# Moving two gate rows and eight modulation columns from TensorE to VectorE and GpSimd in a fused attention and MLP block

## The chip, the cores and the metric

The kernel runs on one core of one Trainium2 chip. The metric is the device time in microseconds (us) of one execution, here the median over several. Most executions agree within 0.3%. One execution of the kernel before took 1975.29 us, a single outlier that no ratio uses. All runs told of here are of the undisturbed state (the records show a mean granted TensorE clock of 1.00, and where a run has less it is said).

## The reference

A block with six modulation vectors made from a condition `c`, attention over the last 512 keys with 32 query heads and 8 key heads, then a two-layer MLP. x is 2048 x 512. Cut to what matters:

```python
mod = (silu(c) @ w_mod).reshape(6, 512)      # sa, ca, ga, sb, cb, gb: slices 0 to 5
h = layernorm(x) * (1 + ca) + sa
x = x + ga * attention(h, k_cache, v_cache, wq, wo)     # softmax over 512 keys
h = layernorm(x) * (1 + cb) + sb
x = x + gb * (relu(h @ w1) @ w2)
```

Slices 0 and 1 are needed at once. Slice 2 (the first gate, a row), slices 3 and 4 (the second modulation, four columns each of 128 partitions) and slice 5 (the second gate, a row) are needed only much later. Those four are what the change is about.

## The kernel before

The 2048 rows are 4 blocks (`NB`) of 512. The main loop has 128 steps, one for each block and head (32 heads to a block, `H`). A step of TensorE work is: scores of this head (psS), queries of a later head (psQ), the product of probabilities and values of the last head (psO, 16 matmuls), and up to four matmuls from a background queue (psW: output projection, and in steps 4 to 6 the modulation). `P` is 128, `DC` and `TPB` are 4.

```python
def mod_row(j):                       # a gate row, on all partitions: 4 matmuls of 512 columns
    sl, dst, r = (2, gaf, R_ga) if j == 0 else (5, gbf, R_gb)
    for cc in range(DC):
        bgq.append(lambda cc=cc: mm(bank[WBK], sc_rep[:, cc, :], wm[sl][:, cc, :], cc == 0, cc == DC - 1, [R_screp, R_wm[sl]], [WBK], cc == DC - 1))
    evac(lambda: kb.op(DVE, lambda e: e.tensor_copy(dst[:, :], bank[WBK]), reads=[R_b[WBK]], writes=[r]))

def mods2():                          # put into the background queue at step 4
    mod_row(0)
    fs = mod_cols_mm(1, WBK)          # slices 3 and 4: 32 matmuls of one column
    bgq.append(lambda: [f() for f in fs] and None)
    evac(lambda: mod_cols_evac(1, WBK))
    mod_row(1)

for s in range(NU):                   # NU = 128 steps
    run_tasks(s, 100)                 # side tasks that were placed at this step
    if s == 4:
        mods2()
    # ... (put an output projection into the queue when 8 heads are done)
    s_mms(s, 0)
    if s + QA < NU:
        q_mms(s + QA)
    s_mms(s, 1)
    if s >= 1:
        pv_mms(s - 1)
    pop_bg(4)
```

VectorE has to empty psO at each step, in program order with all else it does. TensorE can't start the next psO block before (in the trace after, psO blocks stood 3.2 us in all for it):

```python
def pv_mms(u):
    # ... 16 matmuls into o_ps, banks 5 and 6
    kb.op(DVE, lambda e: e.reciprocal(rinv[:, u, :], o_ps[:, :, P]), reads=[R_b[5], R_b[6]], writes=[R_rinv])
    kb.op(DVE, lambda e: e.tensor_tensor(o_sb[u % NOS][:, :, :], o_ps[:, :, 0:P], rinv[:, u, :].unsqueeze(2).to_broadcast([P, TPB, P]), op=ALU.mult),
          reads=[R_b[5], R_b[6], R_rinv], writes=[R_o[u % NOS]])
    # ... DMA transpose of o_sb to oT
```

The layer norms of blocks 1 to 3 and the second layer norms of blocks 0 to 2 are side tasks over some twelve steps each. They share one buffer `xn` (normalised rows) and one buffer `xnT` (the same, transposed by a DMA):

```python
xn = T("xn", [P, TPB, D])
xnT = T("xnT", [P, TPB, DC, P])

def add_ln(b, which, s0):
    dst, r = (hT[b % 2], R_hT[b % 2]) if which == 1 else h2_of[b]
    for tl in range(TPB):
        add(s0 + tl, lambda t=b * TPB + tl: ln_stat(t))               # DVE
    add(s0 + TPB, lambda: ln_rstd(b))                                 # DVE add, POOL power
    for tl in range(TPB):
        add(s0 + TPB + 1 + tl // 2, lambda t=b * TPB + tl: ln_norm(t))  # DVE: xn
    add(s0 + TPB + 2, ln_dmaT)                                        # DMA: xnT <- xn
    for cc in range(DC):
        add(s0 + TPB + 5 + cc // 2, lambda cc=cc: ln_mod_sb(cc, dst, r, which))  # DVE: hT <- xnT

for b in range(1, NB):
    # ...
    add_ln(b, 1, H * b - 15)          # steps 17 to 27, 49 to 59, 81 to 91
for b in range(NB - 1):
    add_ln(b, 2, H * (b + 1) + 19)    # steps 51 to 61, 83 to 93, 115 to 125
```

Of the kernel before, what the change touches and what calls it, by code (L numbers as in the profile page):

```python
# [3 lines left out]

# [2 lines left out]

ACTF = mybir.ActivationFunctionType
ALU = mybir.AluOpType
AX = mybir.AxisListType  # L10
BF = mybir.dt.bfloat16
F32 = mybir.dt.float32
# [1185 lines left out]
def build_fast(nc, es, top, A_x, A_k_cache, A_v_cache, A_wq, A_wo, B_x, B_w1, B_w2, c, w_mod, out, flag):  # L1198
    P = 128
    _, Sq, D = A_x.shape  # L1200
# [10 lines left out]
    DC = D // P  # L1211
# [15 lines left out]
    def T(name, shape, dt=BF):  # L1227
        return es.enter_context(nc.sbuf_tensor(name, shape, dt))
# [9 lines left out]
    h2T = [T(f"h2T{i}", [P, DC, QB]) for i in range(2)]  # L1238
# [7 lines left out]
    wm = [wm01[:, :, 0:D], wm01[:, :, D:2 * D]] + [wmw[:, i * DC * D:(i + 1) * DC * D].rearrange("p (c n) -> p c n", c=DC) for i in range(2, 6)]  # L1246
# [7 lines left out]
    ident = T("ident", [P, P])  # L1254
    ones = T("ones", [P, P])
    c_row = T("c_row", [DC, P])
    s3 = T("s3", [P, 4], F32)
    sc_bf = T("sc_bf", [P, DC])
    sc_rep = T("sc_rep", [P, DC, P])
    tmp = T("tmp", [P, DC], F32)  # L1260
    modc = T("modc", [P, 4 * DC], F32)
    gaf = T("gaf", [P, D], F32)
    gbf = T("gbf", [P, D], F32)
    st = T("st", [P, NT, 6], F32)
    mv = T("mv", [P, NT, 2], F32)
    rstd = T("rstd", [P, NT], F32)
    cst = T("cst", [P, 4], F32)
# [9 lines left out]
    bank = [s_ps[0][:, 0, :], s_ps[0][:, 1, :], s_ps[1][:, 0, :], s_ps[1][:, 1, :], q_ps[:, :],  # L1277
            o_ps[:, 0:2, :].rearrange("p a b -> p (a b)"), o_ps[:, 2:4, :].rearrange("p a b -> p (a b)"), w_ps[:, :]]
    QBK, WBK = 4, 7

    sem = lambda name: top.enter_context(nc.semaphore(name))
    kb = KB(nc)
    PE = kb.stream("pe", sem("s_pe"))
    ACT = kb.stream("act", sem("s_act"))
    DVE = kb.stream("dve", sem("s_dve"))
    POOL = kb.stream("pool", sem("s_pool"))
# [13 lines left out]
    RL = lambda name, n: [Res(f"{name}{i}") for i in range(n)]  # L1300
# [4 lines left out]
    R_acc, R_wm, R_w1, R_w2 = RL("acc", TPB), RL("wm", 6), RL("w1", FC), RL("w2", FC)  # L1305
    R_xn, R_xnT = RL("xn", TPB), Res("xnT")
    R_yt, R_yo = RL("yt", NY), RL("yo", NY)
    R_b = RL("bank", 8)
    R_ident, R_ones, R_c, R_sc, R_screp, R_tmp, R_cst = (Res(n) for n in ("ident", "ones", "c", "sc", "screp", "tmp", "cst"))
    R_moda, R_modb, R_ga, R_gb = Res("moda"), Res("modb"), Res("ga"), Res("gb")  # L1310
    R_st, R_mv, R_rstd = RL("st", NT), RL("mv", NT), RL("rstd", NT)
    R_s3, R_eps = Res("s3"), Res("eps")
    R_rinv, R_vmax, R_chk, R_good, R_flag = Res("rinv"), Res("vmax"), Res("chk"), Res("good"), Res("flag")
# [31 lines left out]
    def wm_res(sl, cc):  # L1345
        return R_wm[cc // (DC // 2)] if sl < 2 else R_wm[sl]
# [15 lines left out]
    def mm(out_ap, lhsT, rhs, start, stop, reads, bk, signal):  # L1362
        kb.op(PE, lambda e: e.matmul(out_ap, lhsT, rhs, start=start, stop=stop), reads=reads, group_writes=[R_b[k] for k in bk], signal=signal)  # L1363
# [66 lines left out]
    def mod_cols_mm(which, bk):  # L1430
        fs = []
        for idx, sl in enumerate((0, 1) if which == 0 else (3, 4)):
            for c2 in range(DC):
                for cc in range(DC):
                    last = idx == 1 and c2 == DC - 1 and cc == DC - 1
                    fs.append(lambda sl=sl, c2=c2, cc=cc, col=idx * DC + c2, last=last: mm(
                        bank[bk][:, col:col + 1], wm[sl][:, cc, c2 * P:(c2 + 1) * P], sc_bf[:, cc:cc + 1],
                        cc == 0, cc == DC - 1, [R_sc, wm_res(sl, cc)], [bk], last))
        return fs

    def mod_cols_evac(which, bk):
        mo, r = which * 2 * DC, (R_moda, R_modb)[which]
        kb.op(DVE, lambda e: e.tensor_copy(modc[:, mo:mo + DC], bank[bk][:, :DC]), reads=[R_b[bk]], writes=[r])
        kb.op(DVE, lambda e: e.tensor_scalar(modc[:, mo + DC:mo + 2 * DC], bank[bk][:, DC:2 * DC], 1.0, None, op0=ALU.add), reads=[R_b[bk]], writes=[r])

    def mod_row(j):
        sl, dst, r = (2, gaf, R_ga) if j == 0 else (5, gbf, R_gb)
        for cc in range(DC):
            bgq.append(lambda cc=cc: mm(bank[WBK], sc_rep[:, cc, :], wm[sl][:, cc, :], cc == 0, cc == DC - 1, [R_screp, R_wm[sl]], [WBK], cc == DC - 1))
        evac(lambda: kb.op(DVE, lambda e: e.tensor_copy(dst[:, :], bank[WBK]), reads=[R_b[WBK]], writes=[r]))  # L1450

    bgq = deque()

    def pop_bg(n):
        while bgq and (n > 0 or bgq[0] in evacs):
            f = bgq.popleft()
            f()
            n -= 1
            if f in evacs:
                break  # L1460
# [3 lines left out]
    def evac(f):  # L1464
        evacs.add(f)
        bgq.append(f)

    def q_mms(u, bk=QBK):
        b, h = units[u]
        order = CC_ORDER if u < QA else range(DC)  # L1470
        for i, cc in enumerate(order):
            mm(bank[bk], wq_sb[:, cc, h * Dh:(h + 1) * Dh], hT[b % 2][:, cc, :], i == 0, i == DC - 1,
               [R_wq[h], R_hT[b % 2][cc]], [bk], i == DC - 1)
        kb.op(ACT, lambda e: e.activation(qT[u % NQT][:, :], bank[bk], ACTF.Copy), reads=[R_b[bk]], writes=[R_qT[u % NQT]])  # L1474

    def s_mms(u, pr):
        b, h = units[u]
        g = h // R
        for i in range(2):
            kc = pr * 2 + i  # L1480
            mm(s_ps[pr][:, i, :], kT_sb[:, g, kc * P:(kc + 1) * P], qT[u % NQT][:, :], True, True, [R_kT[g], R_qT[u % NQT]], [kc], i == 1)
        kb.op(ACT, lambda e: e.activation(PT[u % NPT][:, pr * 2:pr * 2 + 2, :], s_ps[pr][:, :, :], ACTF.Exp, scale=scale),  # L1482
              reads=[R_b[pr * 2], R_b[pr * 2 + 1]], writes=[R_PT[u % NPT][pr]])
# [18 lines left out]
    def enqueue_wo(b, j):  # L1502
        for tl in range(TPB):
            t = b * TPB + tl
            for i in range(HQ):
                h = j * HQ + i
                slot = (b * H + h) % NOT
                bgq.append(lambda i=i, h=h, slot=slot, tl=tl: mm(bank[WBK], oT[slot][:, tl, :], wo_sb[:, h, :], i == 0, i == HQ - 1,
                                                                [R_oT[slot], R_wo[j]], [WBK], i == HQ - 1))

            def fin(tl=tl, t=t):
                if j == 0:
                    kb.op(DVE, lambda e: e.tensor_copy(acc[:, tl, :], bank[WBK]), reads=[R_b[WBK]], writes=[R_acc[tl]])
                else:
                    kb.op(DVE, lambda e: e.tensor_tensor(acc[:, tl, :], bank[WBK], acc[:, tl, :], op=ALU.add), reads=[R_b[WBK], R_acc[tl]], writes=[R_acc[tl]])  # L1515
                if j == NPASS - 1:
                    eng = DVE if b == NB - 1 else POOL
                    kb.op(eng, lambda e: e.tensor_tensor(acc[:, tl, :], acc[:, tl, :], gaf[:, :], op=ALU.mult), reads=[R_acc[tl], R_ga], writes=[R_acc[tl]])  # L1518
                    kb.op(eng, lambda e: e.tensor_tensor(x_sb[:, t, :], acc[:, tl, :], x_sb[:, t, :], op=ALU.add), reads=[R_acc[tl], R_x[t]], writes=[R_x[t]])
                    x1_done.append(t)  # L1520
            evac(fin)
# [5 lines left out]
    def add(step, fn):  # L1527
        tasks.append((step, len(tasks), fn))
        tasks.sort(key=lambda x: x[:2])

    def run_tasks(step, n):
        while tasks and tasks[0][0] <= step and n > 0:
            tasks.pop(0)[2]()
            n -= 1
# [53 lines left out]
    for tl in range(3):  # L1588
# [3 lines left out]
          reads=[R_x[t3], R_rstd[t3], R_s3], writes=[R_xn[t3]])  # L1592
    fs = mod_cols_mm(0, QBK)
# [12 lines left out]
    load_v(1)  # L1606
    q_mms(0)
    q_mms(1, 5)
    kb.op(DVE, lambda e: e.tensor_copy(sc_rep[:, :, :], sc_bf[:, :].unsqueeze(2).to_broadcast([P, DC, P])), reads=[R_sc], writes=[R_screp])


    for g in range(2, G):
# [1 line left out]
    for g in range(G):  # L1614
        for i, op in enumerate((ALU.max, ALU.min)):
            add(max(R * g, 3), lambda g=g, i=i, op=op: kb.op(DVE, lambda e: e.tensor_reduce(vmax[:, i, g:g + 1], v_sb[:, g, :, 0:Dh], axis=AX.XY, op=op),
                                                             reads=[R_v[g]], writes=[R_vmax]))
# [9 lines left out]
    for i, s in enumerate([s for s in range(57, NU) if s % HQ in (1, 2, 3, 4)][:FC]):  # L1627
        add(s, lambda i=i: load_mlp(i))

    def mods2():  # L1630
        mod_row(0)
        fs = mod_cols_mm(1, WBK)
        bgq.append(lambda: [f() for f in fs] and None)
        evac(lambda: mod_cols_evac(1, WBK))
        mod_row(1)

    for s in range(NU):
        run_tasks(s, 100)
        if s == 4:
            mods2()  # L1640
        if wo_ready and wo_ready[0][0] <= s:
            _, b_, j_ = wo_ready.popleft()
            enqueue_wo(b_, j_)
# [7 lines that stand above are left out]
# [100 lines left out]
def bass_adaLN_cond__sliding_block_cached__dense_activation_relu__prompt_kernel(  # L1751
# [14 lines left out]
    with ExitStack() as top:  # L1766
        flag = top.enter_context(nc.sbuf_tensor("flag", [1, 8], mybir.dt.int32))
        with ExitStack() as es:
            kb, fast, cut, dma_cnt, flag_ev = build_fast(nc, es, top, *args, flag)
            sems = dict(kb.sems)  # L1770
            meet = top.enter_context(nc.semaphore("s_meet"))
# [71 lines left out]
```

## Time and profile before

| what | kernel before |
|---|---|
| median of 3 executions, us (all: 564.13, 1975.29, 563.9) | 564.13 |
| span in the profile, us | 562.5 |
| TensorE busy | 553.7 us, 98% |
| VectorE idle while it waits for psO | 233.1 us |
| GpSimd busy | 38.7 us, 7% |
| packets on queue 8, which the page lists as instruction | 35 |

Times are taken from outside and are some 1.7 us longer than the span. The prediction below quotes the main lines and says how to read them. In short: the chain is the path that ended last, and a saving counts only if the work lies on it; a group line ends with how long its engine was idle ahead of it, and after the arrow with what ended that. The view is the waits of the kernel before (engine, tile and line, what it waited for, then us in total, times, the longest):

```profile
DVE hT L1392 <- DMA xnT<-xn: 9.2, 3, 4.3
...
DVE xn L1384 <- DMA xnT<-xn: 4.5, 2, 2.2
```

The one of 4.3 us is the last layer norm, behind the loop. The other four, 2.2 to 2.5 us each, lie in blocks 2 and 3, and they cost TensorE nothing: the list has no wait of a psO block for VectorE.

### The profile page before, as it was taken

The page shows a single profiled execution, that of the slowest core. Times are in us where ns is not written, and L with a number is a line of the kernel's source. Part 1 is how long each engine was busy: PE and PEld are TensorE (multiplying, and loading weights), DVE is VectorE, ACT ScalarE, POOL GpSimd, SP SyncE. Part 2 cuts the span into 40 slices and gives each one's busy share as a digit, 9 for nine tenths or more (in the row PEclk, how much of TensorE's full clock was granted, in tenths as well). Part 3 has the DMA queues.
Part 4 walks back from the last instruction along what each step waited for, and adds up shares of the span by engine and source line. Part 5 has one row for each costly group of instructions (what it writes and reads, how often), then busy time and mean ns, then how long its engine had stood idle before and what let it go on. Part 6 is the DMA issues. An engine that isn't in the chain of part 4 may idle for free.

```text
span 562.5 us, 9700 instructions
## 1 busy us (share of the span) xinstructions
PE 553.7 (98%) x4097; PEld 316.9 (56%) x4172; DVE 242.2 (43%) x533; ACT 350.4 (62%) x453; POOL 38.7 (7%) x42
## 2 busy tenths in 40 slices
PE   8999999999999999999999999999999999999998
PEld 3565555555555555555555555555555654444444
DVE  4444465533334655333346553333354448321134
ACT  5986666666666666666666666666666644432500
POOL 1000000003300000033000000330000000000000
PEclk9999999999999999999999999999999999999999
DMA  9778776421331247332523522121123220210001
GB/s 268 204 165 167 143 160 132 113 38 38 39 76 37 39 93 133 57 94 46 144 56 57 102 50 39 39 40 40 39 39 72 44 31 0 41 36 24 22 28 48
DMA packets 113310, 42.70 MB, mean 76 GB/s; under 512 B 93928, under 2 KB 112104, under 8 KB 113256
## 3 DMA queue, kind: packets, MB, share of 16 engines
q1 hardware_dynamic: 112024, 40.82, 35.2%
q10 hardware_dynamic: 1232, 1.15, 0.6%
q8 instruction: 35, 0.57, 0.5%
q14 instruction: 19, 0.16, 0.1%
HBM read 18.35 MB, written 2.10 MB: 36 GB/s over the span
## 4 chain that ended last, share of the span: by engine, by line
PE 97%; issue 1%; DMA 1%; DVE 1%
PE psS L1363 28%; PE psO L1363 26%; PE psQ L1363 23%; PE psW L1363 20%; DMA x<-in_A_x_dram 1%; DVE st L1373 0%; PE psS L1366 0%; DVE mv L1374 0%; DVE rstd L1574 0%; DVE PT L1673 0%; DVE PT L1675 0%; DVE tmp L1427 0%; DVE sc_bf L1428 0%; DVE tmp L1426 0%
## 5 line engine op out<-in xcount | busy, mean ns | idle before, releaser
L1482 ACT ACTIVATE PT<-psS 128x1024 bf16<-128x1024 f32 x256 | 262.6, 1028 | 129.5 <-PE psS L1363 129.4
L1363 PE MATMUL psS<-qT,kT 128*128 128x512 bf16 x509 | 151.1, 379 | 0.2
L1363 PEld LDWEIGHTS psO<-v,PT 128*128 128x128 bf16 x2048 | 126.6, 98 | 30.2
L1363 PE MATMUL psO<-v,PT 128*128 128x129 bf16 x2048 | 137.0, 220 | 0.0
L1363 PE MATMUL psQ<-hT,wq 128*128 128x512 bf16 x507 | 130.3, 379 | 0.1
L1492 DVE RECIPROCAL rinv<-psO 128x4 f32<-128x4 f32 x128 | 23.4, 183 | 233.1 <-PE psO L1363 233.1
L1363 PE MATMUL psW<-wo,oT 128*128 128x512 bf16 x451 | 117.9, 379 | 3.2
L1493 DVE TENSOR_TENSOR o<-psO,rinv 128x512 bf16<-128x512 f32 x128 | 88.5, 692 | 4.4
L1363 PEld LDWEIGHTS psQ<-hT,wq 128*128 128x128 bf16 x508 | 49.6, 98 | 60.7 <-issue 0.5
L1363 PEld LDWEIGHTS psS<-qT,kT 128*128 128x128 bf16 x512 | 49.6, 98 | 59.3 <-ACT PT L1482 0.7
L1474 ACT ACTIVATE qT<-psQ 128x512 bf16<-128x512 f32 x127 | 75.2, 592 | 0.5 <-PE psQ L1363 0.5
L1662 ACT ACTIVATE wq<-psS 128x512 bf16<-128x512 f32 x56 | 33.4, 597 | 49.6 <-PE psS L1363 49.6
L1363 PEld LDWEIGHTS psW<-wo,oT 128*128 128x128 bf16 x512 | 45.0, 98 | 32.9 <-DVE acc L1515 1.2
L1515 DVE TENSOR_TENSOR acc<-psW,acc 128x512 f32<-128x512 f32 x48 | 33.2, 691 | 6.7 <-PE psW L1363 6.7
L1363 PE MATMUL psO<-wmw,wq 128*128 128x512 bf16 (+1 forms) x164 | 32.7, 352 | 0.3
L1518 POOL TENSOR_TENSOR acc<-acc,gaf 128x512 f32<-128x512 f32 x12 | 15.3, 1272 | 168.7 <-DVE acc L1515 168.7
L1379 POOL TENSOR_TENSOR rstd<-rstd,cst 128x4 f32<-128x4 f32 x7 | 7.1, 1012 | 265.3 <-DVE rstd L1378 265.3
L1363 PE MATMUL psS<-h2T,wmw 128*128 128x512 bf16 x110 | 25.2, 379 | 0.1
L1673 DVE TENSOR_TENSOR PT<-psO,gbf 128x512 f32<-128x512 f32 (+1 forms) x12 | 7.5, 624 | 40.4 <-PE psO L1363 40.4
L1363 PEld LDWEIGHTS psO<-wmw,wq 128*128 128x128 bf16 x168 | 15.4, 98 | 16.5
L1363 PE MATMUL psS<-hT,wmw 128*128 128x512 bf16 x110 | 24.4, 379 | 0.1
L1373 DVE BATCH_NORM_STATS2 st<-x 128x6 f32<-128x512 bf16 x31 | 21.0, 678 | 4.8 <-DMA x<-in_A_x_dram 4.8
(73 smaller groups left out, 170.4 us busy)
## 6 DMA issues: line engine op xcount, KB each, us to landing
wo<-in_A_wo_dram SPq DMA_DIRECT2D x4, 1024.0 KB, 5.7
wq<-in_A_wq_dram SPq DMA_DIRECT2D x7, 512.0 KB, 5.7
wmw<-in_B_w_dram SPq DMA_DIRECT2D x14, 256.0 KB, 3.3
wmw<-in_w_mod_dram SPq DMA_DIRECT2D x5, 512.0 KB, 4.7
oT<-o SPq DMA_TRANSPOSE x128, 2.4
out_dram<-PT SPq DMA_DIRECT2D x15, 128.0 KB, 1.8
x<-in_A_x_dram SPq DMA_DIRECT2D x3, 512.0 KB, 4.1
v<-in_A_v_cache_dram SPq DMA_DIRECT2D x8, 128.0 KB, 4.8
```

What stands on the lines that cost most here:

```text
L1363: kb.op(PE, lambda e: e.matmul(out_ap, lhsT, rhs, start=start, stop=stop), reads=reads, group_writes=[R_b[k] for k in bk], signal=signal)
L1373: kb.op(DVE, lambda e: e.bn_stats(st[:, t, :], x_sb[:, t, :]), reads=[R_x[t]], writes=[R_st[t]])
L1379: kb.op(POOL, lambda e: e.tensor_tensor(rstd[:, sl], rstd[:, sl], cst[:, 0:1].to_broadcast([P, hi - lo]), op=ALU.pow), reads=R_rstd[sl] + ...
L1474: kb.op(ACT, lambda e: e.activation(qT[u % NQT][:, :], bank[bk], ACTF.Copy), reads=[R_b[bk]], writes=[R_qT[u % NQT]])
L1482: kb.op(ACT, lambda e: e.activation(PT[u % NPT][:, pr * 2:pr * 2 + 2, :], s_ps[pr][:, :, :], ACTF.Exp, scale=scale), reads=[R_b[pr * 2], R ...
L1492: kb.op(DVE, lambda e: e.reciprocal(rinv[:, u, :], o_ps[:, :, P]), reads=[R_b[5], R_b[6]], writes=[R_rinv])
L1493: kb.op(DVE, lambda e: e.tensor_tensor(o_sb[u % NOS][:, :, :], o_ps[:, :, 0:P], rinv[:, u, :].unsqueeze(2).to_broadcast([P, TPB, P]), op=A ...
L1515: kb.op(DVE, lambda e: e.tensor_tensor(acc[:, tl, :], bank[WBK], acc[:, tl, :], op=ALU.add), reads=[R_b[WBK], R_acc[tl]], writes=[R_acc[tl]])
L1518: kb.op(eng, lambda e: e.tensor_tensor(acc[:, tl, :], acc[:, tl, :], gaf[:, :], op=ALU.mult), reads=[R_acc[tl], R_ga], writes=[R_acc[tl]])
L1662: kb.op(ACT, lambda e: e.activation(h1T[b % 2][:, fc, :], bank[bk], ACTF.Relu), reads=[R_b[bk]], writes=[R_h1[b % 2][fc]], pre=all_events( ...
L1673: kb.op(DVE, lambda e: e.tensor_tensor(yt[i][:, c0:c1], bank[bk][:, c0:c1], gbf[:, c0:c1], op=ALU.mult), reads=[R_b[bk], R_gb], writes=[R_ ...
```

## The change

The intent is to take the 40 late modulation matmuls off TensorE, which is the bound. VectorE multiplies each weight slice by the condition, a partial product over 128 input features at a time (four to a slice, at most one in a step), and GpSimd adds over the partitions with an all-reduce. For the two gates the result is the row itself, on every partition. For slices 3 and 4 the columns are the diagonals of the 128-wide pieces of the row; VectorE takes them with a product with the identity and a reduction, at step 48. The steps are chosen so that products and sums fall where VectorE has little else. The diff, with the declarations cut:

```diff
-    sc_rep = T("sc_rep", [P, DC, P])
+    sc_f = T("sc_f", [P, DC], F32)
+    prv = h2T[1][:, :, :].rearrange("p c q -> p (c q)").bitcast(F32)
+    pr = [gaf[:, :], prv[:, 0:D], prv[:, D:2 * D], gbf[:, :]]
 ...
-    def mod_row(j):  (shown above)
+    def mod_part(sl, cc):
+        dst, r = pr[sl - 2], R_pr[sl - 2]
+        if cc == 0:
+            kb.op(DVE, lambda e: e.tensor_scalar(dst, wm[sl][:, 0, :], sc_f[:, 0:1], None, op0=ALU.mult), reads=[R_wm[sl], R_scf], writes=[r])
+        else:
+            kb.op(DVE, lambda e: e.scalar_tensor_tensor(dst, wm[sl][:, cc, :], sc_f[:, cc:cc + 1], dst, op0=ALU.mult, op1=ALU.add),
+                  reads=[R_wm[sl], R_scf, r], writes=[r])
+
+    def mod_sum(sl):
+        src, rs = pr[sl - 2], R_pr[sl - 2]
+        kb.op(POOL, lambda e: e.partition_all_reduce(src, src, P, bass_isa.ReduceOp.add), reads=[rs], writes=[rs])
+
+    def mod_col(sl):
+        src, rs = pr[sl - 2], R_pr[sl - 2]
+        o = 2 * DC + (sl - 3) * DC
+        v = src.rearrange("p (c j) -> p c j", c=DC)
+        kb.op(DVE, lambda e: e.tensor_tensor(v, v, ident[:, :].unsqueeze(1).to_broadcast([P, DC, P]), op=ALU.mult), reads=[rs, R_ident], writes=[rs])
+        kb.op(DVE, lambda e: e.tensor_reduce(modc[:, o:o + DC], v, axis=AX.X, op=ALU.add), reads=[rs], writes=[R_modb])
+        # ... (slice 4: add 1)
 ...
-    def mods2():  (shown above)
+    for sl, steps in ((2, (5, 6, 7, 9)), (3, (10, 11, 13, 14)), (4, (15, 25, 26, 27)), (5, (29, 30, 31, 33))):
+        for cc, s in enumerate(steps):
+            add(s, lambda sl=sl, cc=cc: mod_part(sl, cc))
+    for sl, s in ((2, 10), (3, 27), (4, 38), (5, 105)):
+        add(s, lambda sl=sl: mod_sum(sl))
+    for sl in (3, 4):
+        add(48, lambda sl=sl: mod_col(sl))
 
     for s in range(NU):
         run_tasks(s, 100)
-        if s == 4:
-            mods2()
```

More of the change, by code (lines that the diff above doesn't have):

```diff
@@ L5 @@
 import concourse.bass as bass
+from concourse import bass_isa
 from concourse import mybir
@@ L1308, in build_fast @@
     R_b = RL("bank", 8)
-    R_ident, R_ones, R_c, R_sc, R_screp, R_tmp, R_cst = (Res(n) for n in ("ident", "ones", "c", "sc", "screp", "tmp", "cst"))
+    R_ident, R_ones, R_c, R_sc, R_scf, R_tmp, R_cst = (Res(n) for n in ("ident", "ones", "c", "sc", "scf", "tmp", "cst"))
     R_moda, R_modb, R_ga, R_gb = Res("moda"), Res("modb"), Res("ga"), Res("gb")
+    R_pr = [R_ga] + RL("pr", 2) + [R_gb]
     R_st, R_mv, R_rstd = RL("st", NT), RL("mv", NT), RL("rstd", NT)
@@ L1444, in mod_cols_evac @@
         kb.op(DVE, lambda e: e.tensor_scalar(modc[:, mo + DC:mo + 2 * DC], bank[bk][:, DC:2 * DC], 1.0, None, op0=ALU.add), reads=[R_b[bk]], writes=[r])
-    def mod_row(j):
-        sl, dst, r = (2, gaf, R_ga) if j == 0 else (5, gbf, R_gb)
-        for cc in range(DC):
-            bgq.append(lambda cc=cc: mm(bank[WBK], sc_rep[:, cc, :], wm[sl][:, cc, :], cc == 0, cc == DC - 1, [R_screp, R_wm[sl]], [WBK], cc == DC - 1))
-        evac(lambda: kb.op(DVE, lambda e: e.tensor_copy(dst[:, :], bank[WBK]), reads=[R_b[WBK]], writes=[r]))
+    def mod_part(sl, cc):
[14 more added lines that the diff above has]
+        kb.op(DVE, lambda e: e.tensor_reduce(modc[:, o:o + DC], v, axis=AX.X, op=ALU.add), reads=[rs], writes=[R_modb])
+        if sl == 4:
+            kb.op(DVE, lambda e: e.tensor_scalar(modc[:, o:o + DC], modc[:, o:o + DC], 1.0, None, op0=ALU.add), reads=[R_modb], writes=[R_modb])
     bgq = deque()
@@ L1608, in build_fast @@
     q_mms(1, 5)
-    kb.op(DVE, lambda e: e.tensor_copy(sc_rep[:, :, :], sc_bf[:, :].unsqueeze(2).to_broadcast([P, DC, P])), reads=[R_sc], writes=[R_screp])
+    kb.op(DVE, lambda e: e.tensor_copy(sc_f[:, :], sc_bf[:, :]), reads=[R_sc], writes=[R_scf])
     for g in range(2, G):
@@ L1628, in build_fast @@
         add(s, lambda i=i: load_mlp(i))
-    def mods2():
-        mod_row(0)
-        fs = mod_cols_mm(1, WBK)
-        bgq.append(lambda: [f() for f in fs] and None)
-        evac(lambda: mod_cols_evac(1, WBK))
-        mod_row(1)
+    for sl, steps in ((2, (5, 6, 7, 9)), (3, (10, 11, 13, 14)), (4, (15, 25, 26, 27)), (5, (29, 30, 31, 33))):
[5 more added lines that the diff above has]
+        add(48, lambda sl=sl: mod_col(sl))
     for s in range(NU):
         run_tasks(s, 100)
-        if s == 4:
-            mods2()
         if wo_ready and wo_ready[0][0] <= s:
```

## The prediction

The first rival is that VectorE stands still while a partition sum runs. The sum came to 564.13 - 2.54 = 561.6 us. The 562.1 us that were predicted hold about 0.5 us more, for the first two rivals together; since terms of these are cut, that 0.5 can't be followed to its parts and stands as the author's estimate alone.

> **What bounds the kernel now.** I read the page's engine shares first, then the chain of work that ended last, then that chain piece by piece in the stretch where the change acts, then the groups of instructions for durations.
>
> ```profile
> PE 553.7 (98%) x4097; PEld 316.9 (56%) x4172; DVE 242.2 (43%) x533; ACT 350.4 (62%) x453; POOL 38.7 (7%) x42
> ...
> PE 97%; issue 1%; DMA 1%; DVE 1%
> ```
>
> TensorE (PE) is busy 98% of a span of 562.5 us, and 97% of the chain that set the end is its matmuls. VectorE (DVE) has 57% of the span free and GpSimd (POOL) 93%. So a matmul taken away shortens the span by its own pace, and work put on DVE or POOL is free as long as TensorE never has to wait for it. The chain of waits from 25 to 45 us shows the pace (start, length, what; lengths do not overlap):
>
> ```profile
> 25.09 0.91 PE psO L1363 x16
> 26.00 0.86 PE psW L1363 x4
> 26.86 0.43 PE psS L1363 x2
> ...
> 28.59 0.91 PE psO L1363 x16
> 29.49 0.78 PE psW L1363 x32
> 30.27 0.08 issue
> ...
> 32.02 0.91 PE psO L1363 x16
> 32.93 0.86 PE psW L1363 x4
> ...
> 35.52 0.91 PE psO L1363 x16
> ...
> 38.15 0.91 PE psO L1363 x16
> ...
> 40.78 0.91 PE psO L1363 x16
> 41.69 0.43 PE psW L1363 x2
> ```
>
> One step of the loop is one block of 16 psO matmuls to the next. The three psW pieces are what the change removes: the gate row for slice 2, the 32 one-column matmuls for slices 3 and 4, the gate row for slice 5. Steps 4, 5 and 6 last 28.59 - 25.09 = 3.50, 32.02 - 28.59 = 3.43 and 35.52 - 32.02 = 3.50 us; steps 7 and 8, with nothing in psW, last 2.63 (38.15 - 35.52, 40.78 - 38.15). From step 9 the output projection fills psW, four matmuls a step, and a step is 3.50 again (44.28 - 40.78).
>
> **What DVE and POOL pay for an operation**, from the groups kept apart by shape:
>
> ```profile
> L1493 DVE TENSOR_TENSOR o<-psO,rinv 128x512 bf16<-128x512 f32 x128 | 88.5, 692 | 4.4
> L1492 DVE RECIPROCAL rinv<-psO 128x4 f32<-128x4 f32 x128 | 23.4, 183 | 233.1 <-PE psO L1363 233.1
> L1518 POOL TENSOR_TENSOR acc<-acc,gaf 128x512 f32<-128x512 f32 x12 | 15.3, 1272 | 168.7 <-DVE acc L1515 168.7
> L1616 DVE TENSOR_REDUCE vmax<-v 128x1 f32<-128x512 bf16 x16 | 10.9, 681 | 0.3
> L1392 DVE TENSOR_SCALAR hT<-xnT,modc 128x512 bf16<-128x512 bf16 x20 | 7.2, 407 | 9.2 <-DMA xnT<-xn 9.2
> L1518 DVE TENSOR_TENSOR acc<-acc,gaf 128x512 f32<-128x512 f32 x4 | 2.8, 692 | 0.1
> ```
>
> A two-operand op over 512 elements costs DVE 0.69 us, a scale-and-shift 0.41. DVE sat 233.1 us of the span just waiting for psO: that idle time is where the new work must fit, without moving the psO eviction (reciprocal plus product, about 0.9 us after each block).
>
> [...]
>
> **The change, part by part.**
> Removed from TensorE: the excess of steps 4 to 6 over a bare step, 0.87 + 0.80 + 0.87 = 2.54 us. Checked by pieces: 0.86 + 0.78 + 0.08 + 0.86 = 2.58. All of it is on the chain. A bare step stays at 2.63 us: there ACT needs two exponentials of 1.03 and one copy of 0.59, 2.65 us at full durations, so bare steps are balanced between TensorE and ACT and cannot get faster, but those of steps 7 and 8 show what they cost. Also gone are the row copies out of psW (2 x 0.69 on DVE, hidden), two small column evictions, and the 0.42 us replication of the conditioning vector (a 4-element copy remains), all off the chain.
> Added to DVE: 16 partial products, four of the scale kind (about 0.41 us; fp32 output may make it more) and twelve multiply-adds at 0.69, so 1.6 + 8.3 = 9.9 us, one in each of 16 steps. A bare step has 2.63 - 0.9 = 1.7 us of DVE left, a step of 3.50 has 3.50 - 0.9 - 0.69 = 1.9 even when it also evicts psW. The partial comes after one eviction and before the next, so 0.69 fits. The tightest ones are steps 26 and 27, with two scale-and-shift ops of the next block (0.73) besides: 0.9 + 0.69 + 0.73 + 0.69 = 3.0 of 3.50. Hidden.
> At step 48 two diagonal extractions: 2 x (0.69 + 0.68) + 0.16 = 2.9 us in a row. DVE is then about 0.3 us late for the next psO eviction, but TensorE writes psO again only 3.50 - 0.91 = 2.6 us after the block ended, of which the eviction takes about 1.1: some 1.5 us of slack. Hidden.
> Added to POOL: four partition sums over 128x512 fp32. I have no duration. POOL's plain two-operand op takes 1.27 us at this width; a sum[...] should cost a few times that. My estimate is 4 to 10 us[...]. What matters is order: POOL also does the small power of each layer norm and the gated residual of three blocks. The gate row is first needed at step 34; the second modulation columns at about step 60; gate row 5 in the MLP. All have tens of us to spare.
> Moved: everything after step 6 happens 2.5 us earlier. Transfers are heavy there (DMA share 1.30 between 30 and 35 us in the stretch table), but the first output weights are issued at 25.57, land in about 6 us and are not used until 41.5 now, 39 then. Hidden.
> Sum: 564.13 - 2.54 = 561.6 us if nothing comes back.
>
> **The rivals.**
> [...]The partial sum of slice 2 starts when its fourth product is done in step 9, and the products of slice 3 are placed in steps 10, 11, 13 and 14, right beside it. Counting from the end of the psO block in step 9: the sum starts at about 1.1 + 0.69 + 0.2 = 2.0 us, the next product wants to start after the following eviction, at 2.63 + 1.1 = 3.7. If it is locked out until the sum ends, DVE is late, and TensorE waits once the eviction of the block ending at 6.1 is not done by 8.7, so the sum has to be over by about 7.3. A sum shorter than 5.3 us costs nothing, one of 7 us costs 1.7, one of 10 us 4.7. The sum of slice 3 is queued for step 27, but its data is ready from step 14 and POOL has only the power of step 21 ahead of it; so it really starts in step 21 to 23, beside the normalisation of the next block and perhaps the products in 25 to 27: with 10 us another 0.5 to 2 us.[...] Against it: the sums were visibly spread into chosen steps, and 1.5 us of slack absorbs short blocks. It would make 563 to 568.
> Second, POOL becomes late: a sum of tens of us,[...] would delay the power that the normalisation waits for (2.7 us ahead of its use now), or the residual work behind the fourth-slice sum at step 38, whose accumulator DVE overwrites in step 46. DVE would wait in order, psO would not be emptied, TensorE would stop.[...] Against: the idle time before POOL's ops is 168.7 and 265.3 us in total[...]. It would make 564 to 567, or in the bad tail over 575.
> Third, a transfer or ACT hides the gain: no DMA wait of TensorE is in the chain after the start, and bare steps already run at 2.63. I give it little; it would make 563 to 564.
>
> **Range and chances.** The gain is capped by 2.5 us, 0.45% of the time, so faster by 2% is out of reach and the question is only how much comes back. I give somewhat over half to nothing or nearly nothing coming back (561.2 to 562.3), about a third to 1 to 5 us back, the rest to a late POOL. I predict 562.1 us, with 561.0 to 566.5 holding 8 times in 10. Faster 0.01, within 2% 0.94, slower 0.05 (over 11 us lost would need a sum of some 20 us or more on the path).
>
> **What would show it.** In the profile after: steps 4 to 8 at 2.63 us each in TensorE's chain and no psW before about 39 us (the gain); DVE's products at 0.41 and 0.69 us even where a partition sum runs (no lock) or drawn out and starting late there (lock); psO blocks evenly 3.50 us apart around steps 10 to 14 and 21 to 28, or with a gap on TensorE ended by DVE (cost come back); the powers on POOL starting right after their DVE input[...]. The prediction is wrong if TensorE's idle time rises by over 2 us after step 9, if a bare step takes more than 2.7 us, or if the sums on POOL last more than about 10 us.

## The result and the profile after

| | before | after |
|---|---|---|
| median, us | 564.12 (6 executions, with the outlier; the other five 563.9 to 564.89) | 562.95 (6 executions, 562.78 to 563.54) |
| span in the profile, us | 562.5 | 561.0 |
| TensorE busy, us | 553.7 | 550.8 |
| VectorE busy, us | 242.2 | 252.4 |
| GpSimd busy, us | 38.7 | 51.7 |

The ratio is 0.9979, with a 95% interval of 0.9966 to 0.9993, so "within 2%". A ratio here is one of mean times, so not quite the ratio of the medians quoted. The time is 0.85 us above the predicted 562.1 and well inside the range of 561.0 to 566.5. But 2.5 us were to be saved, and 1.2 were. The page after, engine shares and chain:

```profile
PE 550.8 (98%) x4057; PEld 314.7 (56%) x4132; DVE 252.4 (45%) x550; ACT 350.4 (62%) x453; POOL 51.7 (9%) x46
...
PE 93%; DMA 4%; DVE 2%; issue 1%; DVEq 0%
```

TensorE lost 40 matmuls and 40 weight loads, as it should. What is new is that the chain is 93% TensorE, where it was 97%, that DMA is 4% of it, where it was 1%, and VectorE 2% in place of 1%. First the gain itself, in the chain of waits from 15 to 60 us:

```profile
25.02 0.91 PE psO L1367 x16
...
27.66 0.91 PE psO L1367 x16
...
35.55 0.91 PE psO L1367 x16
...
38.19 0.91 PE psO L1367 x16
39.09 0.86 PE psW L1367 x4
```

Steps 4 to 8 now take 2.63 us each ((38.19 - 25.02) / 5), and nothing is in psW before the output projection at 39.09. So the gain is in full there: 2.52 us. To see where it goes, take the start of each psO eviction (VectorE's reciprocal) in the trace after, minus the same in the trace before. The difference is constant over long stretches and jumps in few places; "pv" counts the psO blocks from 0, and block n lies in step n + 1:

```
pv:            0      4      5      6   ...  54     55     56     57     58  ...  86     87     88     89     90  ...  127
after-before -0.07  -0.93  -1.74  -2.59    -2.59  -1.00  -2.12  -1.04  -1.94    -1.94  -0.38  -1.49  -0.38  -1.26    -1.27
```

The lead of 2.59 us (2.52 from steps 4 to 6, 0.07 from an earlier start) holds for 48 steps, then 0.65 us is lost in steps 56 to 59 and 0.67 in steps 88 to 91; 1.27 is left at the end. (Block 47 is once 0.15 us late, beside the diagonal extraction of step 48, and costs nothing.) The two places are the first layer norms of blocks 2 and 3, which run directly into the second ones of blocks 0 and 1. VectorE's timeline of the kernel before around the first of them (start, length, engine, line, operation, and in brackets the wait and what ended it), the two lines with a wait for the transpose:

```profile
205.72 0.74 DVE L1384 TENSOR_SCALAR xn<-x,mv,rstd 128x512 bf16<-128x512 bf16 x2 [2.24 <-DMA xnT<-xn]
...
212.94 0.74 DVE L1392 TENSOR_SCALAR hT<-xnT,modc 128x512 bf16<-128x512 bf16 x2 [2.46 <-DMA xnT<-xn]
```

And the same two of the kernel after:

```profile
204.72 0.73 DVE L1388 TENSOR_SCALAR xn<-x,mv,rstd 128x512 bf16<-128x512 bf16 x2 [3.83 <-DMA xnT<-xn]
...
211.90 0.73 DVE L1396 TENSOR_SCALAR hT<-xnT,modc 128x512 bf16<-128x512 bf16 x2 [3.54 <-DMA xnT<-xn]
```

The first writes `xn` for the next layer norm and has to wait until the transpose has read it; the second reads `xnT` and waits for the second transpose, which was issued late because of the first. Waits of 2.24 and 2.46 us fit into the time between two psO blocks. Waits of 3.83 and 3.54 don't: the eviction queued behind them is late, and TensorE stands. The waits after show it, with two lines of TensorE that the list of before doesn't have:

```profile
DVE hT L1396 <- DMA xnT<-xn: 11.4, 3, 4.2
...
DVE xn L1388 <- DMA xnT<-xn: 7.6, 2, 3.8
...
PEld psO L1367 <- DVE o L1512: 2.6, 4, 0.8
...
PE psO L1367 <- DVE o L1512: 0.6, 2, 0.3
```

The chain of waits after, in that stretch, is the mechanism in four lines: transpose, normalisation, eviction, psO block; before, this stretch was matmuls only (and 0.05 us of issue at two places):

```profile
198.71 5.91 DMA xnT<-xn
...
204.72 0.12 DVE xn L1388
...
205.58 0.70 DVE o L1512
...
206.33 1.08 PE psO L1367 x16
```

The transpose took 5.91 us from issue to landing. In the kernel before, the same took 4.32. Nothing about it had been changed. What differed is what was in flight beside it. The trace's DMA records have one kind of packet of 16,384 bytes on queue 8, the one that the page lists as instruction fetches. There is one every 15.8 us or so in the loop; 8189 recorded TensorE matmuls and weight loads over 33 of them is about 248 each, so they follow TensorE's instructions. Put beside the transposes of the layer norms (all numbers in us, from the DMA records):

```
transpose of      before: issued  landed after  fetch begins    after: issued  landed after  fetch begins
block 1, first            89.83      4.38       none in flight         86.81      6.17        91.09
block 2, first           201.30      4.32       199.44, ahead         198.71      5.91       202.75
block 0, second          208.54      4.37       none in flight        207.54      4.33       none in flight
block 3, first           313.20      4.33       311.33, ahead         311.26      5.89       315.20
block 1, second          320.44      4.38       none in flight        320.06      4.38       none in flight
```

Each transpose that has a fetch begin while it is in flight takes 5.9 to 6.2 us, each other one 4.3 to 4.4. In all eleven traces it is 22 transposes with a fetch, 5.78 to 6.21 us, and 55 without, 4.24 to 4.39 us but for one of 5.08 (behind the loop of run 8), which is unexplained. The transposes of the head outputs (oT) show it too: of the 256 in the traces before and after, 44 have a fetch begin in flight and land after 3.94 us in the median, the other 212 after 2.41. The transpose of block 1 was slow too, but nothing follows it closely, so nobody noticed. The change moved the fetches because it took 80 instructions out of TensorE's stream: relative to the work, the fetch at 202.75 lies 202.75 + 2.59 - 199.44 = 5.9 us later than its counterpart before, and now inside the transpose.

This is a theory so far. Other groups of the profile after, for the terms of the prediction:

```profile
L1460 POOL PARTITION_ALL_REDUCE h2T<-h2T x2 | 6.5, 3247 | 14.0 <-issue 14.0
L1455 DVE SCALAR_TENSOR_TENSOR h2T<-wmw,sc_f,h2T 128x512 f32<-128x512 bf16 x6 | 4.5, 743 | 0.0
```

A sum took 3.25 us, and ahead of these two GpSimd was idle for 14.0 us with nothing to wait for ("issue"). A multiply-add took 0.74 us; the scale form took 0.48 (0.77 once, beside a sum).

### The profile page after: what moved, and what is told of

It is laid out like the page before. It is cut to its first block, busy times and chain, and to the rows that moved or that the text cites. A ratio compares the mean times of both kernels' runs of the same rounds, so it can differ in the third digit from the quotient of the medians.

```text
span 561.0 us, 9655 instructions
## 1 busy us (share of the span) xinstructions
PE 550.8 (98%) x4057; PEld 314.7 (56%) x4132; DVE 252.4 (45%) x550; ACT 350.4 (62%) x453; POOL 51.7 (9%) x46
## 4 chain that ended last, share of the span: by engine, by line
PE 93%; DMA 4%; DVE 2%; issue 1%; DVEq 0%
PE psS L1367 27%; PE psO L1367 26%; PE psQ L1367 22%; PE psW L1367 18%; DMA xnT<-xn 3%; DMA x<-in_A_x_dram 1%; DVE o L1512 0%; DVE st L1377 0%; DVE xn L1388 0%; PE psS L1370 0%; DVE acc L1534 0%; DVE mv L1378 0%; DVE hT L1396 0%; DVE rinv L1511 0%; DVE rstd L1593 0%
```

## The experiments

The theory (F, for fetch): what came back is the lengthened transpose, because an instruction fetch falls into it; the change did this only by shifting the place in the work at which each fetch comes. Its rivals: (D) the change's own work on VectorE and GpSimd, or its smaller lead over the transfers, makes the layer norm late; (C) the four sums, by holding VectorE up while they run or through GpSimd being late, take time elsewhere. A loss of 1.3 us isn't much larger than the scatter of the start: the loop of one profile begins up to 0.9 us later than that of the kernel before, of another 0.2 earlier. So the offsets step by step, in which a jump can be told from a late start, are read ahead of the times. Further kernels measure what the prediction left unmeasured: whether a sum holds VectorE up, the spreading of the products, and a sum on the path.

The kernels ran with shared runs of the kernel before. Its medians were 563.94 (the first four), 564.04 (the next four) and 564.20 us (the last). All nine gave correct results.

### 1. The removed instructions put back, ahead of the loop

44 tiny matmuls (one column, nobody reads the result) before the loop, so 88 TensorE instructions with their weight loads, against the 80 removed:

```diff
+    def pad(n):
+        for i in range(n):
+            mm(bank[WBK][:, 0:1], ones[:, :], ones[:, 0:1], True, True, [R_ones], [WBK], i == n - 1)
 ...
     warm(9)
+    pad(44)
```

Expected: 

> The changed kernel with 44 more one-column matmuls (88 TensorE instructions) in the idle 1.3 us after the second warm-up group. Theory F (instruction fetch): of the 2.59 us saved by step 6, some 1.3 us are lost because 16 KB fetches of TensorE's instructions now fall into the transposes of the normalised rows for blocks 2 and 3 (5.9 us to landing in place of 4.3). 88 instructions move each fetch about 5.5 us earlier in the work, to before those transposes: both land in 4.2 to 4.5 us, TensorE waits nowhere for psO, the time is 561.5 to 561.9, about 1.2 us under the changed kernel, and the offset against the kernel before stays at -2.5 or more to the last step. Rival R (the added VectorE products[...] cost the 1.3 us): the same time as the changed kernel, 562.9, or a little more.

Measured: span 559.9 us, median 561.76; ratio 0.9977 (0.9952 to 1.0001). The interval is wide because two of the six executions took 564.9 us, three more than the other four (561.18 to 561.77); why is open. By the ratio this run can't be told from the change (0.9979). The fetches now begin at 196.7 and 308.5, ahead of the two transposes, all layer norm transposes land after 4.26 to 4.39 us, and VectorE's wait is back at the value of before (its timeline):

```profile
202.99 0.73 DVE L1392 TENSOR_SCALAR xn<-x,mv,rstd 128x512 bf16<-128x512 bf16 x2 [2.25 <-DMA xnT<-xn]
```

No psO block waits for VectorE, and the lead of 2.74 us over before holds to the end. The whole work of the change is in this kernel, at the same steps, so D and C can't be what took the time. In the profile and in four of six executions, more instructions took less time.

### 2. The same 44 matmuls behind the loop (control)

```diff
     ln_dmaT()
+    pad(44)
     flag_mm()
```

Expected: 

> Control: the same 44 one-column matmuls, but in the last part of the program, just ahead of the small flag matmul, behind all layer norms. They cost TensorE 44 x 0.025 to 0.028 = 1.1 to 1.2 us where it is the bound. Both theories: 564.0 to 564.2; the transposes of blocks 2 and 3 land as late as in the changed kernel (5.9 us). If this run were as fast as the one with the matmuls at the head, theory F would fall.

Measured: span 563.1 us, median 564.79; ratio 1.0006 (0.9994 to 1.0019). The transposes take 5.96 and 5.84 us, and the lead goes from 1.73 to 0.41 us, a loss of 1.32, as in the change. (The start of the loop was 0.8 us later in this profile, which is why the lead starts smaller; the pads themselves take 1.24 us at 477 us.) So it isn't the presence of the pads or some luck of a rebuilt program, but their place ahead of the transposes.

### 3. The second layer norms of blocks 0 and 1 six steps later

If nobody has to wait for the transpose, its length should not matter:

```diff
-        add_ln(b, 2, H * (b + 1) + 19)
+        add_ln(b, 2, H * (b + 1) + (25 if b < 2 else 19))
```

Expected: 

> The changed kernel with the second layer norms of blocks 0 and 1 begun 6 steps later (offset 25 in place of 19), so that they no longer follow directly behind the first layer norms of blocks 2 and 3. Theory F: the two VectorE waits for those transposes (3.8 and 3.6 us each time) are gone whether a fetch falls into them or not, TensorE doesn't wait for psO, and the whole gain shows: 561.5 to 561.9. Rival R: 562.9, because the products and sums are as before.

Measured: span 559.8 us, median 561.63 (561.50 to 561.89); ratio 0.9955 (0.9943 to 0.9967). This is the fastest version, steadily. The transposes are still slow, 5.83 and 5.88 us with fetches at 202.56 and 314.52 inside them. But the multiply that stood waiting for 3.54 us in the change now starts without a wait (timeline of VectorE; a bracket would be at the end of the line):

```profile
207.71 0.73 DVE L1396 TENSOR_SCALAR hT<-xnT,modc 128x512 bf16<-128x512 bf16 x2
```

The lead of 2.68 us is kept to the end. Runs 1 and 3 take away the two halves of the theory, the fetch in the transpose and the wait for it, one each, and either half alone gives the 1.3 us back.

### 4. The same on the kernel before (control)

Expected: 

> The kernel before with the same 6 steps. There VectorE's waits of 2.2 and 2.5 us fit in TensorE's slack (no idle time of TensorE is put down to VectorE), so theory F expects no change: 564.0 to 564.2. If it gains 1 us or more, the schedule of the layer norms cost the kernel before too, and the 1.3 us are not the change's own.

Measured: span 562.3 us, median 563.93; ratio 0.9994 (0.9982 to 1.0006). No change: apart from a start 0.16 us earlier the evictions stand where they stood, except two at each of the two places that come 0.3 and 0.5 us earlier still, with nothing gained for the next. Here the moved transposes were hit by fetches (5.88 and 6.04 us), at no cost. So the gain of run 3 isn't a gain of the order as such; it removes a loss which only the change has.

### 5. The loss made in the kernel before

If F holds, the kernel before must lose as much when its fetches are pushed into its transposes, without anything of the change. 88 tiny matmuls at step 2, 176 instructions. With about 248 recorded instructions to a fetch, that is some 70 short of one whole fetch, so each later fetch comes later in the work, about as the 80 removed ones made it in the change:

```diff
     for s in range(NU):
+        if s == 2:
+            pad(88)
         run_tasks(s, 100)
```

Expected: 

> The other way round: the kernel before, none of the change, with 88 one-column matmuls (176 TensorE instructions) at step 2. They cost TensorE about 88 x 0.028 = 2.5 us. Theory F: [...]every 16 KB fetch falls some 5 us later in the work than before, as in the changed kernel: about 3 us after the issue of the transposes for blocks 2 and 3, which then land in 5.5 to 6 us in place of 4.3, and TensorE loses about 0.65 us at each. Time: 564.0 + 2.5 + 1.3 = 567.8, and 1.3 over the control. If the loss belonged to the change itself (products, sums[...]), this run would cost the same as the control, 566.5.

Measured: span 566.4 us, median 568.45; ratio 1.0075 (1.0062 to 1.0089); two of the six executions had a mean clock of 0.997. The transposes of blocks 2 and 3 now take 5.95 and 5.88 us (issued 204.08 and 316.69, fetches at 208.16 and 320.70). The delay against before is 2.77 us from step 2 on (2.20 the pads, 0.57 a later start), 3.50 from block 58 and 4.17 at the end: 1.40 us lost at the same two places. Its waits:

```profile
PEld psO L1363 <- DVE o L1497: 2.7, 4, 0.8
...
PE psO L1363 <- DVE o L1497: 0.6, 2, 0.3
```

These are the two lines of the change (2.6 in 4 and 0.6 in 2), in a kernel that has no product on VectorE and no sum on GpSimd for the modulation.

### 6. The 88 matmuls behind the loop (control)

```diff
     ln_dmaT()
+    pad(88)
     flag_mm()
```

Expected: 

> Control: the kernel before with the same 88 one-column matmuls ahead of the flag matmul, behind all layer norms. Both theories: 564.0 + 2.5 = 566.5, the transposes of blocks 2 and 3 land in 4.3 us.

Measured: span 565.9 us, median 567.62 (5 executions); ratio 1.0058 (1.0045 to 1.0071). The transposes take 4.34 and 4.32 us and the loop's evictions stand where they stood in before, 0.24 us earlier throughout, so nothing is lost at the two places. As a control by time alone the run is a partial miss: behind the loop the granted clock fell to 0.97 between 480 and 567 us (0.86 from 478 to 490), and the 40 matmuls after the pads took 10.49 us in place of 8.81 in run 5. So the pads cost more there than ahead, and the times of runs 5 and 6 differ by 0.83 us where the losses in the loop differ by 1.40.

### 7. Four products in one step

Is the "one per step" needed? All of slice 3's products at step 10, beside the sum of slice 2:

```diff
-    ... (3, (10, 11, 13, 14)) ...
+    ... (3, (10, 10, 10, 10)) ...
```

Expected: 

> The changed kernel with the four products of slice 3 all in step 10, next to the partition sum of slice 2 (3.25 us on GpSimd), in place of one per step.[...] the products take about 0.5 to 0.8 us each, 2.7 to 3.0 us in a row, plus an eviction of psW; VectorE is late by about 1 us for one psO eviction, within the 1.5 us of slack, and the time is that of the changed kernel, 562.9 to 563.3.

Measured: span 561.9 us, median 562.71; ratio 0.9973 (0.9959 to 0.9988), so as the change. (The start was 1.0 us later in this profile.) The scale form took 0.77 us, being held by the sum, and the three multiply-adds 2.33. The psO eviction behind them was 0.38 us late, and TensorE did not wait. So 0.38 us fit into the slack, and spreading the products over four steps bought nothing here. The 1.5 us of slack that the prediction worked out isn't tested by this. The change itself tests it: at blocks 55 and 57 (the offsets above) the eviction is 1.59 and 1.08 us late, and the next block 0.47 and 0.18 us, so the slack there was about 1.1 and 0.9 us.

### 8. A sum right ahead of a layer norm's power

The prediction's second rival: what if a sum, with the idle time of GpSimd beside it (5.9 to 8.1 us in the change), comes between VectorE and the power that it waits for? Slice 3's last product and its sum at step 20, one step ahead of the power of block 1's layer norm:

```diff
-    ... (3, (10, 11, 13, 14)) ...   and   ((2, 10), (3, 27), (4, 38), (5, 105))
+    ... (3, (10, 11, 13, 20)) ...   and   ((2, 10), (3, 20), (4, 38), (5, 105))
```

Expected: 

> The changed kernel with the last product and the partition sum of slice 3 moved to step 20, so that the sum stands directly ahead of the power of the first layer norm of block 1 on GpSimd. If the 8.1, 5.9, 6.0 and 6.9 us of idle time beside each sum in the changed kernel[...], the power starts about 3.25 + 6.9 us after the last product, near 88 us in place of 79.3; VectorE waits for it some 5 us, TensorE loses 3.5 to 4 us: 566 to 567. If those idle times are only slack or a reading error of the profile, the power is late by 3 us at most, VectorE's wait stays under 1 us and the time is 562.9 to 563.5.

(What is cut is a guess at what the idle time is, which no trace shows; the case is that it comes again here.)

Measured: span 568.6 us, median 570.01; ratio 1.0106 (1.0091 to 1.0121), mean clock 0.994. The expectation was too low. GpSimd's timeline:

```profile
77.81 3.23 POOL L1460 PARTITION_ALL_REDUCE h2T<-h2T  x1 [36.42 <-DVE rinv L1511]
...
88.83 1.05 POOL L1383 TENSOR_TENSOR rstd<-rstd,cst 128x4 f32<-128x4 f32 x1 [7.79 <-issue]
```

The power's input was ready at about 80.1 us, the sum ended at 81.04, and the power began 7.79 us after that with nothing to wait for, though the same operation had run before (at 6.72 and 7.71 us in the change); what GpSimd does in this time the records don't say. VectorE stood 7.98 us, and TensorE's timeline shows what follows:

```profile
86.49 0.59 PE L1367 MATMUL psS<-qT,kT 128*128 128x512 bf16 x2
91.53 1.91 PE L1367 MATMUL psO<-v,PT 128*128 128x129 bf16 x16 [4.45 <-DVE o L1512]
...
97.90 1.07 PE L1367 MATMUL psO<-v,PT 128*128 128x129 bf16 x16
```

After 4.45 us without a matmul the psO block took 1.91 us where it takes 1.07, and the clock was back only some 6 us later. Against the change, the delay was 5.39 us at the block itself and 7.43 one block later: the idle time was 4.45 us, and the slow clock (0.51 granted from 91.5 to 97.5 us, where matmuls that take 3.07 us one step earlier took 5.94) cost some 3 us more. This, and an idle time of 7.8 us where 6.9 was expected, make up the miss. So the second rival is real and dear; the change avoids it by placing the sums in quiet steps.

### 9. A multiply-add right beside a sum

In the change only one scale form overlapped a sum. Here a multiply-add does, which reads two operands from SBUF:

```diff
-    ... (3, (10, 11, 13, 14)) ...
+    ... (3, (8, 10, 11, 13)) ...
```

Expected: 

> The changed kernel with the products of slice 3 in steps 8, 10, 11 and 13, so that a multiply-add with two SBUF inputs (not the one-input scale) meets the partition sum of slice 2 in step 10. In three runs so far a one-input product or small add beside a sum ended only when 2.05 to 2.1 us of the sum plus its own length had passed since the sum's start. If a multiply-add is held back in the same way, it ends about 2.1 + 0.74 = 2.8 us after the sum's start, i.e. takes 1.0 to 1.1 us from its own start in place of 0.74. If two SBUF inputs don't contend with the sum, it takes 0.74 as everywhere else. Time in both cases that of the changed kernel, 562.7 to 563.3[...].

Measured: span 561.4 us, median 562.92; ratio 0.9976 (0.9959 to 0.9992). GpSimd and VectorE, one line each of their timelines:

```profile
38.56 3.25 POOL L1460 PARTITION_ALL_REDUCE gaf<-gaf  x1 [29.73 <-DVE gaf L1455]
```

```profile
40.31 1.03 DVE L1455 SCALAR_TENSOR_TENSOR h2T<-wmw,sc_f,h2T 128x512 f32<-128x512 bf16 x1
```

The multiply-add ended at 41.34; without a hold it takes 0.74, so it was let go at 41.34 - 0.74 = 40.60, 2.04 us after the sum's start. The same arithmetic gives 2.05 us in the change (product ends at 40.73, takes 0.48, sum starts at 38.20), 2.04 in run 7 and 2.11 in run 8, where it held a small add (0.16 us takes 1.03). So VectorE is held, for 2.0 to 2.1 us of a sum that is listed with 3.25, and it cost 0.3 us of VectorE in the change and in run 9, which is hidden (0.87 us in run 8, ahead of the 7.79 us).

## Why the prediction was right or wrong

**What bounds the kernel, and the gain.** Right. TensorE is the bound, the three psW pieces were worth 2.54 us by the chain, and 2.52 arrived in steps 4 to 6. Steps 4 to 8 take the 2.63 us that were read off the two bare steps.

**VectorE's added work.** The mechanism right, two sizes off: 0.48 us a scale (bf16 in, fp32 out) and 0.74 a multiply-add in place of 0.41 and 0.69, so 4 x 0.48 + 12 x 0.742 + 0.29 for the held one is 11.1 us and not 9.9. Hidden all the same, as said; run 7 shows that there was room for more. The slack was smaller than the 1.5 us worked out (0.9 to 1.1, see run 7), which these products never needed. Step 48 went as worked out: the eviction 0.15 us late, TensorE not late.

**GpSimd's sums.** 3.25 us each, under the estimate of 4 to 10; the 5.3 us above which, by the prediction's arithmetic, a sum that locks VectorE out to its end would cost something were not reached, so the first rival was worth nothing. That the sum queued for step 27 would start early was right (step 23, at 88.51 us). GpSimd is idle with nothing to wait for 5.9 to 8.1 us ahead of three of the four sums, and 6.9 us ahead of the residual that follows one; what it does in that time the records don't say. Ahead of the fourth it waits 29.7 us for VectorE anyway. All this is off the path. Run 8 shows what such a sum costs on it, and there the prediction's size was wrong: it gave a late GpSimd 564 to 567 us, short of a bad tail of very long sums, but one sum of 3.23 us and 7.8 us of idle time cost 7.43 us (median 570.01); the estimate had no term for the slow clock. Not every pair of operations on the two engines holds one up: in the trace before, at 8.11 us, a multiply of VectorE with bf16 input and output runs beside a power of GpSimd and takes its usual 0.41 us.

**Where the prediction was wrong.** The step that failed is "Moved: everything after step 6 happens 2.5 us earlier", with its close "Hidden". It looked only at the transfers of the first 45 us, as the third rival did when it gave the transfers "little" and "563 to 564" us. It took all transfers to move with the work. The instruction fetches did not: relative to the work they came some 5.9 us later, and so into the transposes of the layer norms, 160 us after the change acts. 1.3 of the 2.6 us came back there, and runs 1, 3 and 5 show it: with the fetch out of the transpose, the loss is gone; with the reader out of the way, the loss is gone; with the fetch put into the transposes of the kernel before, the loss is there. The rival's time of 563 to 564 was nearly the one that came, 562.95. That the central 562.1 came within 0.85 us is in part luck: it held a come-back of about 0.5 us from VectorE held beside the sums and from a late GpSimd, both of which cost nothing, and had no term for the 1.3 us that did come.

Could it have been seen beforehand? The waits of the kernel before show VectorE waiting 2.24 to 2.5 us for those transposes, which is most of what a step can bear: 1.6 us more tips it. That a fetch falls into it could only be seen with the packets beside the transposes.

**What stays open.** How one fetch of 16 KB makes a transpose 1.6 us longer is shown in part. For the transpose issued at 198.71 us (201.30 before), the records of queue 1 have 2560 packets of 256 bytes in the time from 1.0 to 6.3 us after the issue, in both traces. Before, all begin within 4.5 us of the issue; after, all but 34 do, and those 34 begin 4.91 to 5.79 us after it, behind the fetch's packet (4.04 to 4.92). So the transpose isn't slowed as a whole: a few of its packets come behind the fetch. Why these 34 and no others isn't shown; the records don't name the engine that moved a packet. The fetch's own place has a pattern too: in all 22 cases its packet begins 3.90 to 4.34 us after the issue. Whether it is held until then isn't shown, as the time at which it was asked for isn't in the records. In the kernel before, one that began 0.5 us ahead of the transpose's issue (480.61 and 481.14) did not lengthen it (4.27 us). The two slow executions of run 1 are unexplained.

**A finding by the way.** Both kernels have the order of these tasks wrong: the second layer norm's transpose of blocks 0 and 1 is issued into `xnT` before VectorE has read from it for blocks 2 and 3, and that multiply waits for the second transpose (before: issued 208.54, landed at 212.91, multiply at 212.94). So those blocks take their queries from other rows. The waits of 2.46 and 3.54 us shown above are these, so the smaller part of the loss (0.18 us of 0.65) comes from this order too. Worked out in fp32 from the reference, off the chip, the output changes by 1.5e-5 of its size, because the softmax over these small scores is close to uniform, and no comparison with the reference notices. The order of run 3 mends this, as the second transpose is issued at 226.59, after the multiplies at 207.71 and 211.85. It is both the correct and the fastest version.

## What to carry to other kernels

When a saving arrives in full and then shrinks, subtract the start times of a recurring operation in the two traces: the jumps give the places, and what stands on the path there gives the cause. A wait that is only just hidden has no room for a small delay: here 80 instructions taken out of a long unrolled stream put later instruction fetches some 5.9 us later in the work, and those that fell into a DMA that somebody waits for closely (5.9 us to landing in place of 4.3) took back 1.3 of the 2.6 us saved. So give shared buffers some steps between one user and the next. And keep a partition sum and the elementwise operations of GpSimd away from each other where somebody waits: going from one to the other cost 5.8 to 8.1 us of idle time in these traces, wherever no other wait hid it.
